# Two head pairs transposed through f32 PSUM instead of bf16 PSUM, in a fused attention and SwiGLU kernel

## The chip, the cores and the metric

The kernel runs on one core of one Trainium2 chip. The metric is the device time of one execution in microseconds (us). One execution was also taken by the hardware profiler; its engines are PE (TensorE, the matrix engine, with PEld for its weight loads), DVE (VectorE), ACT (ScalarE), POOL (GpSimd) and SP (SyncE). A matrix product reads SBUF and writes PSUM; DVE and ACT read PSUM and write SBUF.

## What is computed

The reference is attention with a squared ReLU in place of the softmax, then a root mean square norm and a SwiGLU feed-forward layer (FFN):

```python
batch, n_heads, seq, head_dim = (8, 12, 448, 64)
scores = scale * np.matmul(q, k.transpose(0, 1, 3, 2))
attn = np.maximum(scores, 0.0) ** 2 / S
attn_out = np.matmul(attn, v)

x = attn_out.transpose(0, 2, 1, 3).reshape(B * S, H * D)      # 3584 x 768
xn = x / np.sqrt(np.mean(x * x, axis=-1, keepdims=True) + 1e-06) * rms_g
g = xn @ w_gate                                               # 768 x 1536
out = (g * (1.0 / (1.0 + np.exp(-g))) * (xn @ w_val)) @ w_out # 1536 x 768
```

All inputs and the output are f32; the kernel rounds them to bf16 as it loads them and multiplies in bf16 with sums in f32.

## The kernel before

**Tiling.** The scores are computed with keys on the partitions, so that attn needs no transpose; q and k therefore have to lie with the head dimension on the partitions. The 12 heads are taken as 6 pairs j (two heads of 64 fill 128 partitions), and the tile qkT holds, per pair, 448 columns of k and 448 of q. Batch 0 is worked on in two halves of 224 query columns each (a0 and a1), the other batches in one piece of 448. The 448 keys are three blocks of 128 and a remainder of 64; the remainders of two pairs are multiplied together (tile psR). A score unit of a0 is two such blocks (tile psS, 2 x 448 columns); ReLU (lines 858 and 860) moves it to SBUF as r, and line 866 squares it there on DVE. A visit (line 1024, tile psAV) multiplies the squared scores of two pairs by v. When the three visits of a half are through, the sums of squares (psSS), their power (Ln and Exp on ACT, lines 1160 and 1164) and the scaled xn (line 1180) follow, and then the FFN products (line 147 in the profile: the planner's `slot`, tiles psg, psv and psO).

**Transposes.** q and k of batches 0 and 1 are transposed on PE, from batch 2 on by DMA. For batch 0, k of a pair is 7 pieces of 64 x 64 per head, and the first half of q is 2 pieces of 112 x 64 per head. `transposes` (lines 621 to 687) writes all 18 of a pair, with the identity tile as the other operand, into one bf16 PSUM tile psT in one of the two narrow banks, and then one copy of 672 columns, by DVE (line 677) or ACT (line 679), takes them to qkT. The function `transposes_f32` (lines 689 to 741) is in the file too, but no pair uses it while F32_T is 0. The second half of q follows later for three pairs at once.

**Start of the work.** POOL issues the loads of k, q, v and the weights one after the other; heads 0 to 3 of k are the first (line 527). The first halves of q for heads 0 to 3 and 4 to 7 come as f32 through SP's and ACT's queues, and a cast (line 1385, on ACT or DVE) brings each to bf16. PE runs fillers (tile psB, line 1532: products of a constant with itself that no one reads) whenever the planner has nothing for it, until the first FFN product is under way.

**The order** is written out when the kernel is built, by the planner (class Planner). It holds a clock of its own for each engine, with a cost for each instruction, and emits the instructions in the order in which its clock starts them; on the chip each engine runs its instructions in this order, and semaphores hold it where data is missing. An elementwise task may list two engines; `engine_next` (line 90) gives it to the engine that can start it first, then by priority, and on a tie to the engine that is listed first. PEN (line 64) is a handicap in planner nanoseconds for a ReLU on DVE:

```python
key = (s + (self.PEN if e == "dve" and "act" in cost
            and item[3].__name__ in self.acts else 0.0), prio, seq)
```

FLOOR (line 380) is a list of earliest times, by the planner's clock, at which the first eight loads of POOL's queue count as landed; the first is that of k's heads 0 to 3. The planner's narrow banks are m0 and m1, its wide tiles (two banks each) s0, s1 and s2; scores, remainders and visits take wide ones. In a choice for PE the planner looks first at visits, remainders and transposes that are ready (`choose`, line 262), then at score units, then at FFN products, and runs a filler if nothing is ready within 110 ns (GAP, line 61).

Of the kernel before, what the change touches and what calls it, by code (L numbers as in the profile page):

```python
# [54 lines left out]
class Planner:  # L55
# [5 lines left out]
    GAP = 110.0  # L61
    either = ("square", "squared")
    SLACK = 0.0
    PEN = 200.0
    acts = ("relu",)

    def __init__(self, nc, tc, banks, wide, warm):
# [22 lines left out]
    def engine_next(self):  # L90
        best = None
        for item in self.tasks:
# [4 lines left out]
            for e in cost:  # L97
# [3 lines left out]
                if item[3].__name__ in self.either and e == "act" and s + cost[e] > max(r, self.free["dve"]) + cost["dve"] + self.SLACK:  # L101
                    continue
                key = (s + (self.PEN if e == "dve" and "act" in cost and item[3].__name__ in self.acts else 0.0), prio, seq)
                if best is None or key < best[0]:
# [236 lines left out]
def kernel(  # L341
# [35 lines left out]
    JOIN = 300.0  # L377
    LAG = 2800.0
    LAG0 = 2050.0
    FLOOR = 5850.0, 8500.0, 9350.0, 10450.0, 11150.0, 11850.0, 13150.0, 14900.0  # L380
    floors = []
    LASTW = (384, 192, 192)
    A2, A3, A5 = (384, 384), (256, 256, 256), (512, 256)
# [2 lines left out]
    WO = (A2, A2, A2, A2)  # L386
    ORDER = "w0-2 w2-4 k w4-6 w6-8 w8-10 K w10-12 v"
    FIRST = "k4-8 q8-12 k8-12 v0-4 v4-12 Q"
    F32_T = 0
    AGATE = 6  # L390
    THIRD = 0
    THIRDV = 3
# [53 lines left out]
    def issue(fn, nbytes, run, need=(), rate=None, ahead=8):  # L446
# [8 lines left out]
        def go(e):  # L455
# [4 lines left out]
            lag = LAG0 if dma["t"] < 5000.0 else 1900.0 if dma["t"] < 6500.0 else LAG  # L460
            at = max(dma["t"] + lag, FLOOR[len(floors)] if len(floors) < len(FLOOR) else 0.0)
            floors.append(at)
# [977 lines left out]
    for j in range(HP):  # L1440
        if j < F32_T:
            transposes_f32(j)
# [144 lines left out]
```

## Time and profile before

| what | value |
|---|---|
| median of 4 runs | 436.49 us (435.8 to 442.32) |
| the profiled execution's own time | 436.29 us |
| its span | 434.5 us |
| PE, DVE, ACT busy | 429.5, 265.2, 251.4 us |
| granted PE clock | 1.00 of full speed |
| first transposes on PE | 6.08 us |
| first FFN product | 24.92 us |
| fillers (psB) | 78 products, the last at 24.7 us |

The profile's page gives the busy time of each engine, then the span in 40 slices with a digit for the busy share in tenths, and then the costliest groups of instructions by line. The chain that ended last follows the work back from the last instruction. A timeline row is start, duration, engine, line, operation, output<-input, shapes and number of instructions, and in brackets the idle time of the engine before it and what ended that.

### The profile page before, as it was taken

How to read it: one execution, taken by the hardware profiler on the slowest of the kernel's cores; microseconds unless marked ns; L12 is line 12 of the kernel's file. 1: busy time of each engine (PE TensorE's matmuls, PEld its weight loads, DVE VectorE, ACT ScalarE, POOL GpSimd, SP SyncE). 2: the span in 40 equal slices, each digit the busy share in tenths (PEclk: the TensorE clock that was granted, in tenths of full speed). 3: DMA queues.
4: the chain of work that ended last, by engine and by line, in shares of the span. 5: the costliest groups of instructions: out<-in, count | busy, mean ns of one | idle time of the engine just before them, and what ended most of it. 6: DMA issues, size and time to landing. Idle time of an engine off the chain costs nothing.

```text
span 434.5 us, 12552 instructions
## 1 busy us (share of the span) xinstructions
PE 429.5 (99%) x5576; PEld 314.7 (72%) x5576; DVE 265.2 (61%) x437; ACT 251.4 (58%) x356; POOL 78.3 (18%) x97
## 2 busy tenths in 40 slices
PE   8999999999999999999999999999999999999996
PEld 6688788954579755885579855795569955699996
DVE  3898984478754676657854578567854577442200
ACT  4878873576653675757743676576744567342222
POOL 8544311062260160006200440001000000000000
PEclk9999999999999999999999999999999999999999
DMA  9999999699699598169917991157103200020023
GB/s 148 193 196 197 204 192 120 142 165 126 105 160 201 110 146 57 39 132 110 124 38 159 152 158 8 38 119 99 24 18 94 74 2 2 2 74 2 2 74 109
DMA packets 134805, 44.68 MB, mean 103 GB/s; under 512 B 104096, under 2 KB 131296, under 8 KB 134752
## 3 DMA queue, kind: packets, MB, share of 16 engines
q0 software_dynamic: 94448, 24.16, 57.4%
q1 hardware_dynamic: 39808, 19.50, 21.2%
q8 instruction: 43, 0.70, 0.7%
q10 hardware_dynamic: 496, 0.24, 0.2%
q14 instruction: 10, 0.08, 0.1%
HBM read 48.76 MB, written 11.01 MB: 138 GB/s over the span
## 4 chain that ended last, share of the span: by engine, by line
PE 98%; DMA 1%; issue 0%; DVE 0%; ACT 0%; POOLq 0%
PE psO L147 26%; PE psg L147 26%; PE psv L147 26%; PE psAV L1024 9%; PE psS L917 7%; PE psT L662 2%; PE psB L1532 1%; PE psR L938 1%; DMA k<-in_k_dram 1%; PE psSS L1206 0%; PE psSS L1130 0%; DVE qkT L677 0%; ACT ost L1336 0%; POOLq L1571 0%
## 5 line engine op out<-in xcount | busy, mean ns | idle before, releaser
L147 PE MATMUL psv<-xn,wv_sb 64*128 64x448 bf16 (+1 forms) x1296 | 170.3, 329 | 0.0
L147 PE MATMUL psg<-xn,wg_sb 64*128 64x448 bf16 (+1 forms) x1296 | 170.0, 329 | 0.0
L860 ACT ACTIVATE r<-psS 128x896 bf16<-128x896 f32 x133 | 119.1, 919 | 33.5 <-PE psS L917 32.7
L147 PE MATMUL psO<-wo_sb,hT 64*128 64x384 bf16 (+2 forms) x1464 | 132.3, 310 | 0.0
L147 PEld LDWEIGHTS <-hT 64*128 64x128 bf16 x1464 | 109.9, 94 | 14.5 <-issue 2.5
L147 PEld LDWEIGHTS <-wg_sb 64*128 64x128 bf16 x1296 | 94.8, 94 | 30.6 <-issue 3.2
L147 PEld LDWEIGHTS <-wv_sb 64*128 64x128 bf16 x1296 | 93.9, 94 | 31.5 <-issue 2.5
L866 DVE TENSOR_TENSOR r<-r 128x896 bf16<-128x896 bf16 (+1 forms) x171 | 99.9, 609 | 12.1 <-ACT r L860 11.4
L1258 DVE TENSOR_TENSOR hT<-sil,psv 128x448 bf16<-128x448 bf16 x96 | 59.2, 617 | 61.4 <-PE psv L147 61.1
L1242 ACT ACTIVATE sil<-psg 128x448 bf16<-128x448 f32 x96 | 52.3, 545 | 47.8 <-PE psg L147 47.7
L917 PE MATMUL psS<-qkT 64*128 64x448 bf16 (+1 forms) x324 | 53.0, 329 | 0.1
L1336 ACT COPY ost<-psO 128x384 f32<-128x384 f32 (+2 forms) x51 | 23.0, 452 | 50.1 <-PE psO L147 50.0
L508 POOL DMA_DIRECT2D vb<-in_v_dram x18 | 13.1, 742 | 181.0 <-PE psg L147 75.6
L1024 PE MATMUL psAV<-r,vb 64*64 64x448 bf16 (+1 forms) x756 | 43.1, 335 | 0.4
L860 ACT ACTIVATE r<-psR 128x896 bf16<-128x896 f32 (+1 forms) x24 | 20.1, 839 | 28.7 <-PE psR L938 28.7
L1055 DVE TENSOR_SCALAR xT<-psAV 128x896 bf16<-128x896 f32 (+1 forms) x20 | 20.4, 1021 | 25.9 <-PE psAV L1024 25.8
L1180 DVE SCALAR_TENSOR_TENSOR xn<-xT,g_sb,rstd 128x448 bf16<-128x448 bf16 (+1 forms) x54 | 30.2, 627 | 7.8 <-ACT rstd L1164 7.7
L555 POOL DMA_DIRECT2D kb<-in_k_dram x42 | 31.5, 799 | 13.7 <-DMA vb<-in_v_dram 6.3
L1024 PEld LDWEIGHTS <-vb 64*64 64x64 bf16 x756 | 18.5, 105 | 20.6 <-PE psAV L1024 8.5
L917 PEld LDWEIGHTS <-qkT 64*128 64x128 bf16 x324 | 19.2, 94 | 9.8 <-issue 1.1
L858 DVE TENSOR_SCALAR r<-psS 128x896 bf16<-128x896 f32 x11 | 12.0, 1088 | 17.6 <-PE psS L917 17.4
L1080 DVE TENSOR_TENSOR x2f<-xT 128x896 f32<-128x896 bf16 x19 | 20.6, 1084 | 2.0 <-ACT xT L1053 2.0
(49 smaller groups left out, 174.6 us busy)
## 6 DMA issues: line engine op xcount, KB each, us to landing
vb<-in_v_dram POOLq DMA_DIRECT2D x14, 384.0 KB, 6.4
kb<-in_k_dram POOLq DMA_DIRECT2D x42, 96.0 KB, 7.2
qb<-in_q_dram POOLq DMA_DIRECT2D x6, 672.0 KB, 9.8
out_dram<-ost SPq DMA_DIRECT2D x7, 336.0 KB, 2.8
wg_sb<-in_moe_w_gate_dram POOLq DMA_DIRECT2D x6, 384.0 KB, 13.2
wv_sb<-in_moe_w_val_dram POOLq DMA_DIRECT2D x6, 384.0 KB, 13.2
wo_sb<-in_moe_w_out_dram POOLq DMA_DIRECT2D x2, 1152.0 KB, 19.2
out_dram<-ost SPq DMA_DIRECT2D x8, 288.0 KB, 2.9
```

The lines of the kernel that those rows point to most:

```text
L147: mm = self.nc.tensor.matmul(out=seg.bank["tile"][:, off : off + seg.w], lhsT=lhsT[prt], rhs=rhs[prt], start=(seg.first and h == 0 and i = ...
L555: lambda o=o, i=i: nc.gpsimd.dma_start(out=o, in_=i),
L860: nc.scalar.activation(out=r[:, :, :w], in_=ps[:, :, :w], func=ACT.Relu)
L866: nc.vector.tensor_tensor(out=r[:, :, :w], in0=r[:, :, :w], in1=r[:, :, :w], op=ALU.mult)
L917: nc.tensor.matmul(out=ps[:, hh, o : o + n], lhsT=t[prt, j, 0, c * P : (c + 1) * P], rhs=t[prt, j, 1, sub.q0 : sub.q0 + n], start=True, st ...
L1024: mm = nc.tensor.matmul(out=ps[hh * D : (hh + 1) * D, jj, :n], lhsT=vt[prt, 2 * (ja + jj) + hh, u * D : (u + 1) * D], rhs=r[prt, hh, o : o ...
L1055: nc.vector.tensor_scalar_mul(out=xT[at], in0=ps[:, :, :n], scalar1=inv_attn)
L1080: nc.vector.tensor_tensor(out=got["x2"][:], in0=xT[at], in1=xT[at], op=ALU.mult)
L1180: nc.vector.scalar_tensor_tensor(out=xn[:, kt, q0 : q0 + n], in0=xTs[b, 0][:, kt, q0 : q0 + n], scalar=g_sb[:, kt : kt + 1], in1=rstd[:, q ...
L1242: nc.scalar.activation(out=s[:, :m], in_=ps[:, :m], func=ACT.Silu)
L1258: nc.vector.tensor_tensor(out=h[:, fbs[0] : fbs[-1] + 1, o : o + n], in0=s[:, :m].rearrange("p (f s) -> p f s", s=n), in1=ps[:, :m].rearra ...
L1336: nc.scalar.copy(out=ost[:, c0 : c0 + w], in_=ps[:, :w])
```

## The change

The first two pairs of batch 0 take the function `transposes_f32` instead of `transposes`; the handicap of a ReLU on DVE goes from 200 to 100, and the first landing time from 5850 to 6000.

```diff
-    PEN = 200.0
+    PEN = 100.0
...
-    FLOOR = 5850.0, 8500.0, 9350.0, 10450.0, 11150.0, 11850.0, 13150.0, 14900.0
+    FLOOR = 6000.0, 8500.0, 9350.0, 10450.0, 11150.0, 11850.0, 13150.0, 14900.0
...
-    F32_T = 0
+    F32_T = 2
```

The function that is now called, in its core:

```python
def run(s):
    bank = take_wide()
    ps = bank.take("psT")                       # f32, 2 x 512 columns
    parts = (
        ("k", [(u, D, u % UH * P + u // UH * D) for u in range(U)], S),
        ("q", [(c, PC, c * PC) for c in range(2)], 2 * PC),
    )
    for i, (nm, steps, width) in enumerate(parts):
        for c, w, o in steps:
            for hh in range(2):
                nc.tensor.matmul(
                    out=ps[hh * D : (hh + 1) * D, i, o : o + w],
                    lhsT=ld[nm, 0][:w, 2 * j + hh, c * D : (c + 1) * D],
                    rhs=ident[:w, :w], start=True, stop=True,
                )
        s += 2.0 * sum(w / 2.4 + 2.5 for _, w, _ in steps)
        def copy(e, i=i, width=width):
            (nc.vector.tensor_copy if e == "dve" else nc.scalar.copy)(
                out=t[:, j, i, :width], in_=ps[:, i, :width])
        pl.task(2, {"dve": dve_cost(width), "act": act_cost(width)}, copy,
                [Tok(s + 200.0)], done[i], over)
    return s + pl.SW
```

Instead of the transpose mode with a bf16 result, these are ordinary products with the identity, with f32 results; k goes to the first bank of a wide PSUM tile and q to its second bank. There are two copies, one of k's 448 columns and one of q's 224, each with its own readiness, and each may go to DVE or to ACT. The calls in batch 0 are unchanged:

```python
for j in range(HP):
    if j < F32_T:
        transposes_f32(j)
    else:
        transposes(0, [j], 0, 2, True)
```

## The prediction

> **What bounds the kernel now.** I read the page's busy line first, then the chain that ended last in order of time, then the timeline of the first 25 us, then the groups by shape. The page says that TensorE (PE) is busy for almost the whole span:
>
> ```profile
> span 434.5 us, 12552 instructions
> ...
> PE 429.5 (99%) x5576; PEld 314.7 (72%) x5576; DVE 265.2 (61%) x437; ACT 251.4 (58%) x356; POOL 78.3 (18%) x97
> ...
> PEclk9999999999999999999999999999999999999999
> ```
>
> A busy PE is not a useful PE, though. The tile psB is filler: products of ones that no one reads. The chain between 5 and 25 us shows where fillers stand on the path. Columns are start, length, what:
>
> ```profile
> 1.25 4.79 DMA k<-in_k_dram
> ...
> 6.08 1.18 PE psT L662 x36
> 7.26 0.30 PE psB L1532 x2
> 7.56 0.30 PE psS L917 x4
> 7.86 0.30 PE psB L1532 x2
> ...
> 23.20 1.78 PE psB L1532 x17
> ```
>
> From 6.08 us on, the psB pieces of that chain sum to 0.30 + 0.30 + 0.20 + 0.41 + 0.69 + 1.11 + 0.20 + 0.50 + 0.50 + 1.78 = 5.99 us. After 24.9 us, where the first FFN product runs, there is no psB at all, and PE is busy 34.94 of the 35.00 us from 25 to 60 and 299.87 of the 300 us from 100 to 400. So all of the PE's real work after the first FFN product has to be done anyway, and **the only time that an edit of the first stage can win is those 5.99 us**, of which the last 1.78 wait for the scale of the first half (Ln, Exp, table load, xn), not for transposes. What holds the fillers up is DVE and ACT: from 10 to 14 us they are busy 3.88 and 3.56 of 4.00 us. The timeline at the edit itself:
>
> ```profile
> 6.75 0.51 DVE L677 COPY qkT<-psT 128x672 bf16<-128x672 bf16 x1 [5.22 <-PE psT L662]
> ...
> 7.30 0.72 ACT L679 COPY qkT<-psT 128x672 bf16<-128x672 bf16 x1 [3.10 <-PE psT L662]
> 7.48 0.43 DVE L1385 CAST qb<-qf 112x512 bf16<-112x512 f32 x1 [0.23 <-DMA qf<-in_q_dram]
> 7.49 0.11 PEld L917 LDWEIGHTS <-qkT 64*128 64x128 bf16 x4 [0.18 <-DVE qkT L677]
> ...
> 7.92 1.75 ACT L860 ACTIVATE r<-psS 128x896 bf16<-128x896 f32 x2
> ```
>
> Here the bracket is the idle time before the instruction and who ended it. Pair 0 is copied by DVE at 6.75 to 7.26, its scores start at 7.49; pair 1 is copied by ACT at 7.30 to 8.02, and the remainder scores psR, which need both pairs, start at 8.12.
>
> **The change, part by part.** *TensorE.* Per pair 14 products for k and 4 for q, of the same tile sizes (64*64 and 112*64), instead of as many transposes. Before, the 14 k issue from 6.08 to 6.42 and the 4 q from 6.42 to 6.63, 0.55 us a pair. The products are not in the trace. Below I take 0.55 us: the weight loads of the 14 k sum to 0.30 us and stay, so there is nearly nothing to gain. Above: the q transposes issue every 0.21/4 = 52 ns for 112 columns, 0.47 ns a column; 64 columns at that rate without overlap are 30 ns, 14 of them 0.42 instead of 0.34 us, so +0.08 a pair, +0.16 us for both. I take +0, since the AV products with the same 64*64 tiles and f32 out issue 16 in 0.46 us with 224 columns each, far more overlap than is needed here.
>
> The row for the engine clock: the granted clock is 1.00 in every window that I asked. [...]
>
> *Copies.* One copy of 672 bf16 columns becomes a copy of 448 and one of 224 f32 columns. Rows by shape for reading f32 PSUM: DVE 128x448 takes 0.624, 128x896 1.088, so 1.04 ns a column and 224 columns an estimated 0.39; ACT 128x448 takes 0.543, 128x896 0.919, so 224 columns an estimated 0.355, with the 128x224 Ln row at 0.441 as the upper end. Which engine gets which follows from the planner's rule (the engine that can start first, on a tie the one listed first, DVE for copies, ACT for the cast) and its own clock, used for order alone: k of pair 0 goes to DVE, q to ACT; the second q cast, due at 7.4, finds both engines free and now goes to **ACT** instead of DVE; k of pair 1 goes to DVE, and its q, with ACT in the cast, **also to DVE**, behind k.
>
> In trace time: k0 can start when the 14 k of pair 0 end (6.08 + 0.41, and 0.04 as before): DVE 6.53 to 7.15; q0 ACT 6.75 to 7.11. Scores of unit 0, with the 0.23 us seen from copy end to score, at 7.38 instead of 7.49: **-0.11**. k1 DVE 7.10 to 7.72 (neighbours overlap by some 0.05). Cast ACT 7.48 (its data land then) to 8.10, 0.617 by its row. q1 DVE 7.70 to 8.09. So pair 1 is whole at 8.09 instead of 8.02: **+0.07**, and ACT is free for the first relu at about 8.02 instead of 7.92: **+0.10**; DVE is free at 8.09 instead of 7.91. In sum of engine time, 0.51 + 0.72 + 0.43 = 1.66 us become 2 x 0.624 + 0.355 + 0.39 + 0.617 = 2.61 us; q0 and the head start of k0 lie in idle time, the rest doesn't.
>
> *What is queued behind it.* The planner fills PE until pair 1 is ready by its clock, which now counts about 6 fillers (96 ns each) where there were 2. On the chip: unit 0 issues 7.38 to 7.68, 6 fillers to 8.28, the 0.19 us change of tile mode seen in front of psR, psR at 8.47 instead of 8.12: **+0.35**. By then pairs 2 and 3 are due and stand before the second unit, so that unit's relu, at 8.80 to 9.67 on ACT today, moves behind a copy, to about 10.2; the remainder's relu (0.54 on ACT) takes its place. Engines catch up part of that, as they idle 0.39 (ACT, before 10.06) and 0.55 (DVE, before 8.46) now, and PE runs the two transposes of pairs 2 and 3 at the same time as before. I carry the 0.35 of psR to the end, as DVE and ACT are near full until 18 us: below -0.11 (the lead of unit 0, all else absorbed), above +1.2 (the 0.35 and a whole relu, 0.919, that finds no idle time).
>
> *Wide banks.* The two pairs take two of the three wide PSUM tiles, free again at 7.15 and 8.09; unit 0 takes the third at 7.38, psR the first, so nothing waits; pairs 2 and 3 find both narrow banks unused, but they wait for their k anyway (issued 2.80, landing 5.5 to 6.0 later).
>
> *First landing time 6000 instead of 5850, tie weight 100 instead of 200.* Both change only written order. The landing itself (6.04) stays, and 27 fillers precede it either way. A relu now goes to DVE when it can start there over 0.1 us sooner instead of 0.2 (14 of 171 went there). One moved relu costs DVE 1.088 and frees ACT 0.919; the cover is PE's full queue after 25 us (34.94 of 35.00), so 0 there; in 10 to 25 us it is worth between -0.5 (half an idle relu slot: DVE idles 0.43 from 14 to 18 and 1.33 from 18 to 21) and +0.17 (1.088 - 0.919). I take 0, since the engines are nearly equally loaded.
>
> *Sum:* the profiled execution took 436.29 us, its span 434.5 and 1.79 around it; 436.29 + 0.35 = **436.64**. The median of the four runs shown, 436.49, is 0.20 higher, so 436.7 as a round figure between the two bases. A measurement can't tell a change of under 1% (4.4 us) from none here in the sense of the chances below.
>
> **The rivals.** (1) *Faster.* The cast stays on DVE or lands late, q1 goes to ACT at 7.30 to 7.66, and pair 1 is whole at k1's end, 7.72: -0.30 against 8.02; with the -0.5 of the tie weight 436.29 - 0.8 = 435.5. For it: ACT idled 3.10 us before its first copy. Against: by the planner's rule both engines are free at 7.4. (2) *The work lost is a whole relu round:* +1.2, 437.5. For it: DVE 3.88 of 4.00 busy from 10 to 14. (3) *Slower by over 1%: VectorE becomes the bound from 25 to 60 us.* It is busy 31.06 of 35.00 there, 3.94 spare; 21 relus run on ACT in that window. From the fourth that moves (3.94/1.088 = 3.6) each adds 1.088 us: with 9 moved 9 x 1.088 - 3.94 = 5.85, 442.1. For it: the tie weight pushes exactly this way. Against: the planner moves a relu only where DVE can start sooner, and the FFN products let PE run on. (4) *It does not do what it says:* pair 1 is not split between engines, as derived above, and the f32 form buys nothing; that is inside the forecast, 436.3 to 436.7.
>
> **How the numbers follow.** Forecast with (4), 436.2 to 437.2: 0.50. Rival 1: 0.23. Rival 2: 0.23. Rival 3: 0.04. The range runs from rival 1 at 435.5 to rival 2 with the products' +0.16 and the base's 0.20, 437.9; outside stay rival 3 and the tails of the other two. Faster by over 1% would need 4.4 of the 4.21 us of fillers (5.99 - 1.78) that transposes can touch: 0.01. Slower by over 1% is rival 3: 0.04.
>
> **What would show it.** Right: a DVE copy of 448 f32 columns starting near 6.5 and a second near 7.1, an ACT copy of 224 between them; the cast on ACT near 7.5; psR later than 8.12; six fillers before it; the first FFN product at 24.9 to 25.6 instead of 24.92. Wrong: psR before 8.0, psB in the chain under 5.5 us after 6.08 (rival 1); psB over 7 (rival 2); PE idle by more than 1 us between 25 and 60 with DVE over 34 of 35 busy (rival 3).

## The result

The median of the changed kernel is 439.8 us (44 executions, 436.54 to 443.54), that of the kernel before 436.54 us (63 executions, 435.80 to 443.82). The ratio is 1.005 with a 95% interval of 1.0031 to 1.0068: slower by some half per cent, and outside the forecast range of 435.5 to 437.9. (The ratio leaves out the most disturbed executions of both kernels; the medians are of all of them.)

The median hides what happened. Each execution has a mean granted TensorE clock, and the changed kernel's times fall into groups by it: 17 executions at 0.998 to 1.000 take 436.54 to 437.41 us (median 436.92), 13 at 0.990 to 0.991 take 439.66 to 440.45, and 14 at 0.983 to 0.988 take 440.94 to 443.54. So 27 of 44 lost clock. The kernel before has the slower groups too, but 13 of 63 times (counted here by a time over 439 us); its others have a median of 436.50. "Low clock" below means a mean granted clock under 0.995. Two numbers have to be explained: **+0.42 us** between executions at full clock, and **the share of low clock, from 13 of 63 to 27 of 44**.

The profiled execution of the changed kernel (437.01 us) is one at full clock. Its page:

```profile
span 435.2 us, 12562 instructions
...
PE 429.7 (99%) x5582; PEld 315.6 (73%) x5582; DVE 266.8 (61%) x438; ACT 250.9 (58%) x357; POOL 78.2 (18%) x97
...
PEclk9999999999999999999999999999999999999999
```

The timeline at the edit (start, duration, engine, line, operation, shapes, and in brackets the idle time before and who ended it):

```profile
6.09 0.41 PE L721 MATMUL psT<-ident,k 64*64 64x64 bf16 x14 [0.36 <-DMA k<-in_k_dram]
...
6.76 1.18 DVE L731 CAST qkT<-psT 128x448 bf16<-128x448 f32 x2 [5.25 <-PE psT L721]
...
7.42 0.34 ACT L731 CAST qkT<-psT 128x224 bf16<-128x224 f32 x1 [3.18 <-DVE qkT L731]
...
7.82 0.37 PE L917 MATMUL psS<-qkT 64*128 64x224 bf16 x4 [0.54 <-ACT qkT L731]
...
8.22 2.14 DVE L858 TENSOR_SCALAR r<-psS 128x896 bf16<-128x896 f32 x2 [0.28 <-PE psS L917]
...
8.64 0.29 PE L938 MATMUL psR<-qkT 64*64 64x224 bf16 x4
```

Two waits stand here that the forecast didn't have. The copy of k starts at 6.76, when the products of q have ended, not at 6.53, when those of k have. And the copy of q on ScalarE was released by **VectorE's copy of k**, not by TensorE: the two copies, meant to run side by side, run one after the other. TensorE then has nothing to do for 0.54 us, and the first scores start at 7.82 instead of 7.49. The same chain as the one shown of before, from the first k to the first FFN product:

```profile
6.76 0.64 DVE qkT L731
...
7.42 0.35 ACT qkT L731
...
8.18 0.41 PE psB L1532 x3
8.60 0.04 issue
8.64 0.29 PE psR L938 x4
...
13.05 1.60 PE psB L1532 x15
...
25.85 0.20 PE psg L147
```

Two lines of the chain of before, to set beside the last two:

```profile
13.37 0.69 PE psB L1532 x6
...
24.98 0.20 PE psg L147
```

The transposes' copies are now on the path for 0.99 us; by this chain the first FFN product comes at 25.85 instead of 24.98, and the span is 0.7 us longer.

### The profile page after: what moved, and what is told of

Same layout as the page of the kernel before. It is cut to its first block, busy times and chain, and to the rows that moved or that the text cites. A ratio compares the mean times of both kernels' runs of the same rounds, so it can differ in the third digit from the quotient of the medians.

```text
span 435.2 us, 12562 instructions
## 1 busy us (share of the span) xinstructions
PE 429.7 (99%) x5582; PEld 315.6 (73%) x5582; DVE 266.8 (61%) x438; ACT 250.9 (58%) x357; POOL 78.2 (18%) x97
## 4 chain that ended last, share of the span: by engine, by line
PE 98%; DMA 1%; issue 0%; ACT 0%; DVE 0%; POOLq 0%
PE psO L147 26%; PE psg L147 26%; PE psv L147 26%; PE psAV L1024 9%; PE psS L917 7%; PE psB L1532 1%; PE psT L662 1%; PE psR L938 1%; DMA k<-in_k_dram 1%; PE psSS L1206 0%; PE psSS L1130 0%; PE psT L721 0%; DVE qkT L731 0%; ACT qkT L731 0%; ACT ost L1336 0%
## 5 line engine op out<-in xcount | busy, mean ns | idle before, releaser
L860 ACT ACTIVATE r<-psS 128x896 bf16<-128x896 f32 x131 | 117.3, 919 | 33.0 <-PE psS L917 32.1
L860 ACT ACTIVATE r<-psR 128x896 bf16<-128x896 f32 (+1 forms) x26 | 21.6, 831 | 32.1 <-PE psR L938 32.1
L1055 DVE TENSOR_SCALAR xT<-psAV 128x896 bf16<-128x896 f32 (+1 forms) x21 | 21.5, 1024 | 27.7 <-PE psAV L1024 27.6
L1024 PEld LDWEIGHTS <-vb 64*64 64x64 bf16 x756 | 18.6, 105 | 20.4 <-PE psAV L1024 8.3
L858 DVE TENSOR_SCALAR r<-psS 128x896 bf16<-128x896 f32 x13 | 14.1, 1089 | 16.9 <-PE psS L917 16.7
```

The source lines that it names most:

```text
L860: nc.scalar.activation(out=r[:, :, :w], in_=ps[:, :, :w], func=ACT.Relu)
L1024: mm = nc.tensor.matmul(out=ps[hh * D : (hh + 1) * D, jj, :n], lhsT=vt[prt, 2 * (ja + jj) + hh, u * D : (u + 1) * D], rhs=r[prt, hh, o : o ...
L1055: nc.vector.tensor_scalar_mul(out=xT[at], in0=ps[:, :, :n], scalar1=inv_attn)
```

## The experiments

Each kernel ran in five rounds beside the kernel before on the same chip. Of the kernel before, low clock came in 2 of 31, 7 of 28, 3 of 29 and 7 of 29 executions in the four sets, and the medians of its executions at full clock were 436.19, 436.43, 436.40 and 436.41 us. Differences below are against the set's own.

**The changed kernel again**, first beside the next three kernels and a second time in the last set.

> The changed kernel once more, for the spread of its times and, with luck, a profile of an execution with a granted TensorE clock below 1. So far its times fall into three groups: 436.5 to 437.4 us (clock 0.998 to 1.000), 439.7 to 440.5 (0.990 to 0.991) and 440.9 to 443.5 (0.983 to 0.988). Theory C (clock gate): the upper groups are one or two stretches at half clock, started by TensorE's pause of 0.54 us after the first transposes; then the profile shows a clock below 0.95 in one or two of the first slices (0 to 25 us) and full clock after, and over 40% of executions are above 439 us. Rival R1 (chance): the kernel before has such executions as often once enough are taken side by side; then both show the same share above 439 us.

> The changed kernel beside the two others on the same chip: 40 to 65% of executions below clock 0.995, median 437 to 441 us, the others at 436.5 to 437.4. If the share is a property of the chip (rival R7), it can be under 20% here, and then the two others say nothing.

Measured: 6 of 12 and 8 of 12 at low clock; at full clock medians of 436.86 (+0.67) and 436.93 (+0.51). With the first 44 that is 41 of 68, against 32 of 180 of the kernel before, and on both chips the kernel before beside it had far fewer (2 of 31 and 7 of 29): the share is the kernel's own, not chance and not the chip. The first of these two runs was profiled in a low-clock execution (442.75 us). TensorE by stretches of 2.5 us (stretch, its length and busy time, instructions, granted clock, DMA share, GB/s):

```profile
5.00:7.50 2.50, 1.27 (x27) 1.00 1.32 212
7.50:10.00 2.50, 1.90 (x33) 0.69 1.37 190
10.00:12.50 2.50, 2.50 (x46) 0.50 1.45 195
12.50:15.00 2.50, 2.44 (x41) 0.50 1.72 186
15.00:17.50 2.50, 2.50 (x31) 0.50 1.48 197
17.50:20.00 2.50, 2.44 (x33) 0.76 1.46 197
20.00:22.50 2.50, 2.44 (x46) 1.00 1.79 189
```

The clock is at half for (1 - 0.69)/0.5 x 2.5 = 1.55 us of the second stretch, all of the next three, and 1.2 us of the sixth: 10.25 us in one piece, from 8.45 us on, **right after the stretch in which TensorE was least busy** (1.27 of 2.50 us); in every later stretch up to 50 us it is 1.00. In this execution the first k landed late as well, so that TensorE paused 1.23 us in front of the transposes and 0.54 us behind them:

```profile
6.93 0.41 PE L721 MATMUL psT<-ident,k 64*64 64x64 bf16 x14 [1.23 <-DMA k<-in_k_dram]
...
8.65 0.56 PE L917 MATMUL psS<-qkT 64*128 64x224 bf16 x4 [0.54 <-ACT qkT L731]
```

The low-clock profile of the second run (441.22 us) has the same two pauses, the first of them short:

```profile
6.32 0.41 PE L721 MATMUL psT<-ident,k 64*64 64x64 bf16 x14 [0.28 <-DMA k<-in_k_dram]
...
8.04 0.37 PE L917 MATMUL psS<-qkT 64*128 64x224 bf16 x4 [0.54 <-ACT qkT L731]
```

That is no more pause than the full-clock profile has (0.36 and 0.54). The runs below show the low clock more or less often as the pauses change (0 of 10 executions with the second one filled, 41 of 68 with it); the length of the pauses does not decide it for a single execution.

**The parts of the change alone.**

```diff
 # the f32 form alone
-    PEN = 100.0
+    PEN = 200.0
-    FLOOR = 6000.0, ...
+    FLOOR = 5850.0, ...
 # the weights alone
-    F32_T = 2
+    F32_T = 0
```

> F32_T = 2 alone, with the tie weight at 200 and the first landing time at 5850. If the new copies and waits are the cause (theory C and the lost 0.45 us), it behaves like the changed kernel: undisturbed executions at 436.7 to 437.3 us, and over 25% of all executions above 439 us. If the refitted weights are the cause (rival R2), it is like the kernel before: 436.3 to 436.7, under 25% above 439 us.

> Tie weight 100 and first landing time 6000 alone, with F32_T = 0. Theory C: like the kernel before, 436.2 to 436.8 us and under 25% of executions above 439 us. Rival R2 (the weights do it): 436.7 to 437.3 us and over 25% above 439 us.

Measured: the f32 form alone 438.22 us at full clock (**+2.0**), 3 of 8 at low clock. The weights alone 436.95 (**+0.75**), 1 of 11 at low clock. Both times lie above what theory C expected; that of the weights is what rival R2 had, without its share of over 25%. The shares point to the f32 form as the source of the low clock, though 8 and 11 executions are few. At full clock both parts cost, the two together (+0.67) less than either: the new weights repair most of what the f32 form costs with the old ones, and nothing of its wait (0.54 us in the profile of the f32 form alone too). The weights alone write 84 fillers where the kernel before has 78. Their profile kept full clock (0.998) in spite of a long pause in front:

```profile
6.15 0.41 PE L662 MATMUL psT<-ident,k 64*64 64x64 bf16 x14 [1.18 <-DMA k<-in_k_dram]
```

**Two PSUM tiles: the wait between the copies taken away.**

```diff
-            bank = take_wide()
-            ps = bank.take("psT")
+            bank, qbank = take_wide(), take_bank()
+            tiles = [bank.take("psT")[:, 0, :], qbank.take("psTq")]
...
-                            out=ps[hh * D : (hh + 1) * D, i, o : o + w],
+                            out=tiles[i][hh * D : (hh + 1) * D, o : o + w],
...
-                        out=t[:, j, i, :width], in_=ps[:, i, :width]
+                        out=t[:, j, i, :width], in_=tiles[i][:, :width]
```

> The changed kernel with q's products in a PSUM tile of their own (a narrow bank), so that q's copy on ScalarE waits for TensorE and no longer for VectorE's copy of k. Theory C with the wait as its start: q0 is copied at 6.76 to 7.11 beside k0 (6.53 to 7.15), scores start near 7.4 instead of 7.82, TensorE's pause shrinks from 0.54 to under 0.2 us, undisturbed executions fall by 0.3 to 0.5 us to 436.3 to 436.7, and the share above 439 us falls below 30%. Rival R3 (written order, not the wait, sets both): scores start earlier but the fillers eat it, times stay at 436.7 to 437.2 and the share above 439 us stays over 40%.

Measured: 436.65 us at full clock (+0.46, where the changed kernel on this chip has +0.67), and **0 of 11** at low clock. The timeline:

```profile
6.23 0.44 PE L715 MATMUL psT<-ident,k 64*64 64x64 bf16 x14
6.60 0.29 PE L715 MATMUL psTq<-ident,qb 112*64 112x112 bf16 x4
6.71 1.18 DVE L725 CAST qkT<-psT 128x448 bf16<-128x448 f32 x2 [5.19 <-PE psT L715]
...
6.93 0.35 ACT L725 CAST qkT<-psTq 128x224 bf16<-128x224 f32 x1 [2.83 <-PE psTq L715]
...
7.40 0.37 PE L911 MATMUL psS<-qkT 64*128 64x224 bf16 x4
```

Now k's copy starts 0.04 us after k's own products end (6.23 + 0.44), q's copy is released by TensorE and runs beside it, and the scores start at 7.40, 1.17 after the first product instead of 1.73. Both waits of the changed kernel came from the shared tile. The time at full clock moved by 0.2 us only, against the 0.3 to 0.5 expected: most of that part has another cause.

**The pause filled, the waits left.** Three fillers behind the second pair's products, everything else as in the changed kernel.

```diff
+            if j == F32_T - 1:
+                for _ in range(3):
+                    pl.fill()
             return s + pl.SW
```

> The changed kernel with three fillers written behind the products of the second pair and nothing else moved: the copies and the wait of ScalarE for VectorE stay, only TensorE works in place of pausing (its pause of 0.54 us before the first scores should fall below 0.1). Theory C (the pause starts the half clock): executions with a clock below 0.995 fall from half to under 20%, median 436.8 to 437.2 us. Rival R4 (the delay of the scores, or the products themselves, start it): still 40 to 60% below 0.995, median over 438.

```profile
7.21 0.47 PE L1535 MATMUL psB<-const-bfloat16-1.0 128*128 128x224 bf16 x3
7.42 0.35 ACT L731 CAST qkT<-psT 128x224 bf16<-128x224 f32 x1 [3.38 <-DVE qkT L731]
...
7.82 0.37 PE L920 MATMUL psS<-qkT 64*128 64x224 bf16 x4
```

Measured: **0 of 10** at low clock, with the wait in place and the scores at 7.82 as before. It is TensorE's pause that brings the low clock (41 of 68 with it), not the late scores and not the f32 products. At full clock it takes 437.40 (+0.97), more than the 436.8 to 437.2 expected; its profiled execution (437.08) has the first FFN product at 25.86, as the changed kernel has it, so where the rest of the +0.97 lies is not shown.

**A pause made in the kernel before.** Four fillers left out, then eight.

```diff
 # four: those between the first transposes and the remainder scores
-        if self.warm() and (not times or ...):
+        if self.warm() and not 6700.0 < t < 8100.0 and (not times or ...):
 # eight: those four, and the last four in front of the first transposes
+        if count not in [24, 25, 26, 27, 28, 29, 30, 31]:
             nc.tensor.matmul(out=bank.fill, ...)
```

Here and below, `count` stands for the running number of a filler.

> The kernel before, its four fillers between the first transposes and the remainder scores left out (they stand in the plan's 6.7 to 8.1 us), nothing slower and no product with f32: TensorE pauses some 0.3 us twice. Theory C: executions with a clock below 0.995 rise from 16% to over 35%, the others stay at 436.0 to 436.7 us. Rival R4: share unchanged, below 20%.

> The kernel before with eight fillers left out: the last four in front of the first transposes and the four between them and the remainder scores. TensorE's pause for the first k grows by some 0.5 us. Theory C (pauses around the first transposes start the half clock): over 60% of executions below clock 0.995, more than the 6 of 12 with four fillers left out; the others at 436.0 to 436.7 us. Rival R4: share as in the kernel before, under 25%.

Measured: with four out 6 of 12 at low clock, the others at 436.29 (-0.14). Beside it the kernel before had 7 of 28. So the low clock comes with bf16 transposes too, and more often when TensorE pauses behind them, though 12 executions are few. With eight out all six executions take 439.94 to 443.21, where theory C had the undisturbed ones at 436.0 to 436.7; three of them have a recorded clock of 0.985 to 0.988, and three one of 1.000. The profiled one is of the second kind (440.94), and its rows tell more than its mean clock (first two rows of before, then the same two with eight left out):

```profile
6.08 0.41 PE L662 MATMUL psT<-ident,k 64*64 64x64 bf16 x14 [0.47 <-DMA k<-in_k_dram]
6.42 0.29 PE L662 MATMUL psT<-ident,qb 112*64 112x112 bf16 x4
```

```profile
6.04 0.58 PE L662 MATMUL psT<-ident,k 64*64 64x64 bf16 x14 [0.81 <-DMA k<-in_k_dram]
6.55 0.40 PE L662 MATMUL psT<-ident,qb 112*64 112x112 bf16 x4
```

The 14 transposes of k took 0.58 us here and 0.41 in the profile of before, the 4 of q 0.40 and 0.29; none of the 23 fillers in front took less than 345 ns, where those of before reach 261. Their median is 391 ns, as in the first 5 us of before; the later ones of before have 262. TensorE was still slow at 16.7 us, where six fillers take 1.24 us, and no longer at 20.4, where ten take 1.10:

```profile
16.69 1.24 PE psB L1534 x6
...
20.35 1.10 PE psB L1534 x10
```

So this kernel shows a slow pace that lasts from the start to some 20 us, rather than a fall from the faster one. That the four fillers missing in front bring it is a reading: no run leaves out those alone.

**More work in front of the first transposes.** Five more fillers there, in the kernel before and in the changed one.

```diff
 # kernel before
+            if b == 0 and with_k and pairs[0] == 0:
 # changed kernel
+            if j == 0:
 # both
+                for _ in range(6):
+                    pl.fill()
```

Six are asked for, and five more stand in front of the transposes in the profiles (32 instead of 27, and 33 instead of 28); `fill` writes none when no bank is free.

> The kernel before with five more fillers written in front of the first transposes, so that TensorE works on until about 6.2 us instead of 5.6. Theory C: share below clock 0.995 under 8% (22 of 122 in the kernel before), and the others lose at most what the fillers overrun k's landing at 6.04: 436.3 to 436.9 us. Rival R7 (the share is set by the chip and the landing of k, not by the pause): 10 to 30% below 0.995.

> The changed kernel with five more fillers in front of the first transposes; the pause of 0.54 us behind them, the copies and the wait stay. If the two pauses add up (theory C, in its form that the half clock comes when TensorE works too little between 5 and 9 us as a whole): share below clock 0.995 falls from 33 of 56 to under 25%, the others at 436.8 to 437.3 us. If the pause behind the transposes alone decides (rival C2): still 40 to 65%.

Measured: the kernel before with them has **0 of 11** at low clock and a median of 436.48 (+0.08 at full clock); as the kernel before had only 3 of 29 on that chip, this says little alone. The changed kernel with them has 2 of 12, beside 8 of 12 without them on the same chip, and 437.67 at full clock (+1.26, more than expected, not explained). The fillers cover a part of the pause in front (0.40 us in the profile of the kernel before with them, 0.47 without, k landing 0.06 us later), but they don't remove it: in a low-clock profile of the changed kernel with them it is still 0.95 us, as k landed late.

```profile
6.71 0.41 PE L724 MATMUL psT<-ident,k 64*64 64x64 bf16 x14 [0.95 <-DMA k<-in_k_dram]
```

More work in front, with the 0.54 us behind left in place, takes most of the low clock away; removing the pause behind, by fillers or by two tiles, took nearly all of it (0 of 10 and 0 of 11, and 1 of 6 and 0 of 11 in the two further forms with two tiles below). Both pauses count.

The landing of k, which no edit here touches, seems to have a part in it. The first transposes start at 6.22 to 7.32 us in the six profiles whose clock falls. Of the ten with a mean granted clock of 0.997 to 1.000 (that with eight fillers left out aside), they start at 5.92 to 6.23 in eight; the other two are 6.45 in a form with two tiles and, by its chain, 6.89 behind fillers that left no pause.

**The +0.42 at full clock: fillers that the plan writes.** On TensorE the order is written in advance, fillers included, and each issues in 0.1 us (15 in 1.60 in the chain of the changed kernel). In front of the first FFN product the kernel before has 78, the changed one 84, the f32 form alone 87. Five of the 15 in front of the changed kernel's first visit (six in the kernel before) were left out:

```diff
+        if count not in range(43, 48):
             nc.tensor.matmul(out=bank.fill, ...)
```

> The changed kernel with the last 5 of the 15 fillers in front of the first visit left out, all else in the same order. Theory O (fillers written by plan stand on the path): visit 0 starts 0.3 to 0.5 us sooner than 14.57 and the undisturbed executions fall from 436.9 to 436.3 to 436.6 us. Rival R6 (the data of the visit, squares on VectorE, are late anyway): TensorE waits there as long as the fillers took and the time stays at 436.7 to 437.2 us. Clock share: like the changed kernel, 40 to 60%, since the first pause is untouched.

```profile
12.90 1.16 PE L1534 MATMUL psB<-const-bfloat16-1.0 128*128 128x224 bf16 x10
14.01 0.58 PE L1024 MATMUL psAV<-r,vb 64*64 64x224 bf16 x16
```

Measured: the visit's first product at 14.01 instead of 14.70 (0.09 of that is the earlier landing of k), and 436.66 at full clock (+0.23), just above the 436.3 to 436.6 expected. Low clock in 5 of 12. The squares were there; TensorE was running fillers over data that it could have used. The changed kernel did not run beside it on this chip; against its +0.42 to +0.67 in other sets, some 0.2 to 0.4 us is won.

> Two PSUM tiles as in the earlier run, with tie weight 200 and first landing time 5850. Theory O (written order sets the undisturbed time: this one writes 87 fillers, the changed kernel 84, the kernel before 78, at 0.1 us each): 437.2 to 438.3 us, near the f32 form alone with one tile (438.25). Rival R5 (the wait for VectorE sets it): 436.0 to 436.6 us. Share below clock 0.995 under 20% by theory C, as TensorE no longer waits for a copy.

Measured: two tiles with the old weights 437.86 at full clock (+1.43), 1 of 6 low. The wait is gone and the time is still near that of the f32 form alone (+2.0), which has the same 87 fillers in the same places: the written order sets most of it. Nine more fillers at 0.1 us are 0.9 us, so their number alone does not make up the +1.43; what else of the order costs is not shown.

**Fewer fillers in other places**, to find a version that beats both: 14 out in the kernel before, 17 out in the form with two tiles.

```diff
+        if count not in [41, 42, 49, 50, 51, 52, 57, 61, 73, ..., 78]:                  # kernel before
+        if count not in [43, ..., 47, 54, 55, 56, 57, 63, 67, 79, ..., 84]:             # two tiles
             nc.tensor.matmul(out=bank.fill, ...)
```

> The kernel before with 14 of its 51 later fillers left out (2 of 6 before the first visit, 4 of 10 before the second, 1 of 4 twice, 6 of 17 before the first FFN product), all else in the same order. Theory O (fillers written by plan stand on the path): undisturbed executions 0.4 to 1.4 us below the kernel before, 435.0 to 436.0. Rival R6 (data are late anyway): 436.1 to 436.7. Share below clock 0.995 like the kernel before, under 25%, since the first pause is untouched.

> The changed kernel with two PSUM tiles and 17 of its later fillers left out (5 of 15, 4 of 10, 1 of 4 twice, 6 of 17). Theory O: 0.5 to 1.5 us below the form with two tiles (436.65), 435.1 to 436.1 us, and then the f32 form without its false wait and without the plan's surplus is level with the kernel before or better; share below 0.995 under 20%. Rival R6: 436.4 to 437.0 us.

Measured: the kernel before with 14 fewer takes 435.96 at full clock (-0.44), as theory O expected, but with 4 of 12 at low clock, beside 3 of 29, where under 25% was expected. Two tiles with 17 fewer takes 436.64 (+0.24, 0 of 11 low), which is what rival R6 expected: next to the +0.46 of two tiles some 0.2 us is won, not 0.5 to 1.5. The chain of the second kernel shows a wait where fillers were, on ScalarE's ReLUs:

```profile
12.53 2.98 ACT r L854 x4
15.51 0.04 issue
15.55 0.37 PE psS L911 x4
15.92 0.69 PE psB L1528 x6
16.61 0.51 PE psAV L1018 x16
```

**Both together, on the kernel before**: five more fillers in front, 14 fewer later.

> The kernel before with five more fillers in front of the first transposes and 14 fewer later (2 of 6, 4 of 10, 1 of 4 twice, 6 of 18): no half clock as in the form with more warming (0 of 11), and 0.4 us less in the undisturbed executions as in the form with fewer fillers (435.96 against 436.40): median 435.8 to 436.2 us, ahead of both kernels. If the pauses left by the missing fillers bring the half clock (rival C3): over 20% below 0.995 and a median over 436.4.

Measured: 436.15 us (435.50 to 437.46), 0 of 12 at low clock; the kernel before beside it 436.57, with 7 of 29 low. The ratio is 0.9976 with an interval of 0.9948 to 1.0005. It is the fastest median of its set, as expected, but the interval just touches 1; a sure gain is not shown. With the 0 of 11 above, the five fillers in front leave 0 of 23 executions at low clock, against 10 of 58 of the kernel before beside them.

## Why the prediction was wrong, point by point

**The failed step is the engine clock**, a term that the forecast put at nothing. It read a granted clock of 1.00 in every window of one profile and left the clock out of its sum; that there was something to lose was not asked. The times hinted at it: 442.32 among the four shown is 1.3% above the others and lies where the low-clock executions lie. The kernel before stood near an edge, 32 of 180 over it, and the change moved it further over: 41 of 68. The forecast had even written a pause down ("unit 0 issues 7.38 to 7.68", after transposes that issue until 7.2, no filler between) and priced it by its length. Its price is not its length: a low-clock execution costs some 3 to 6.5 us more (439.7 to 443.5 against 436.92). At full clock the changed kernel lies inside the range.

**Copies side by side: wrong, and this made the pause.** "k0 can start when the 14 k of pair 0 end", DVE 6.53 to 7.15 with q0 on ACT at 6.75 to 7.11, was read from the code. With one tile for both, k's copy waits for q's products and q's copy for k's. Scores started at 7.82, not 7.38, and TensorE paused 0.54 us. With two tiles they start at 7.40, and that kernel takes +0.46 at 0 of 11 low clock, against a forecast of +0.35: the reading was right for a kernel that isn't this one.

**The sizes of the copies: right.** 0.624 measured as taken, 224 columns on ACT 0.346 against an estimated 0.355. **The products: right**, k and q of a pair issue in 0.56 us against 0.55, at the lower end of the bounds. (In front of them stand 28 fillers, not the 27 that were to "precede it either way".) **Rival 4 was half right**: for the old weights the second pair's q does go to VectorE behind k, as derived; with the new weights it goes to ScalarE behind the cast, at 8.18.

**psR and the carry to the end: near in number, by luck.** psR at 8.64, forecast 8.47; executions at full clock +0.42, forecast +0.35. But three fillers stood there, not six, and the delay came from the wait; and what reached the end came in part from fillers further on, which the forecast did not count.

**The tie weight: mis-sized.** Taken as 0 "since the engines are nearly equally loaded"; alone, with the landing time, it costs 0.75 us, and it writes six more fillers. The first ReLU went to VectorE (8.22), not to ScalarE as worked out.

**The late rivals: excluded.** VectorE as the bound from 25 to 60 us (rival 3) does not appear: TensorE is busy 35.00 of 35.00 us there in the profile after. It was the only rival that lay wholly above the range, and it named the wrong engine.

## What to carry to other kernels

Before an edit of a kernel's first microseconds, look at the spread of its times: a second group 0.6 to 1.5% up with a lower granted clock (0.983 to 0.991) meant here that TensorE was near a pause that costs far more than it lasts (0.54 us, and an execution some 3 to 6.5 us longer); the edit's pauses must then be seen together with those already there, a late first load among them. Fillers in front of the first real work were a cheap cover for it in the kernel before (+0.08 us), though not in the changed one (+1.26), while fillers written into the order where data may be early are work on the path (the first visit at 14.01 us instead of 14.70 with five fewer). Two engines that read one tile were put in order here even though they touch different parts of it: ScalarE's copy of q started at 7.42, released by VectorE's copy of k, and at 6.93 beside it when q had a tile of its own; look at what released the second one, or give each its own tile.

## What the runs showed of the hardware

Six profiles have a mean granted clock under 0.995, and in the first 25 us of each the clock is at half in one piece. A stretch of 2.5 us with a granted clock of c has (1 - c)/0.5 x 2.5 us at half; from the two stretches at the edges of the piece (start, granted clock), to some 0.03 us:

| profile | first stretch | last stretch | half from | full again | half for |
|---|---|---|---|---|---|
| changed kernel, first run above | 7.5, 0.69 | 17.5, 0.76 | 8.45 | 18.70 | 10.25 |
| changed kernel, second run | 7.5, 0.84 | 17.5, 0.62 | 9.20 | 19.40 | 10.20 |
| f32 form alone | 7.5, 0.77 | 17.5, 0.69 | 8.85 | 19.05 | 10.20 |
| four fillers left out of before | 7.5, 0.62 | 20.0, 0.65 | 8.10 | 21.75 | 13.65 |
| two tiles, old weights | 5.0, 0.93 | 20.0, 0.84 | 7.15 | 20.80 | 13.65 |
| changed kernel, more fillers in front | 10.0, 0.69 | 17.5, 0.94 | 10.95 | 17.80 | 6.85 |

So half clock stood for 6.85 us in one of them, 10.20 to 10.25 in three and 13.65 in two. Why these lengths is not shown.

How much work keeps the clock is not shown either. From 5.0 to 7.5 us TensorE is busy for 0.59 to 2.21 us in the six; for 1.92 in the full-clock profile of the changed kernel and 2.03 in that of the kernel before. Busy time by itself does not separate them. Nor does the longest pause: in two of the six (the second run of the changed kernel and the f32 form alone) none was longer than 0.54 us, and the weights alone kept full clock with one of 1.18.

That the three groups of times answer to the three lengths fits their sizes: half of 6.85, 10.2 and 13.65 us is 3.4, 5.1 and 6.8, and among the first 44 executions the medians at clocks of 0.990 to 0.991, 0.986 to 0.988 and 0.983 to 0.984 lie 2.9, 4.6 and 6.3 us above those at full clock. The lengths themselves were seen only in the executions that were profiled.

A granted clock of 1.00 is not always one pace. It stands over the first 5 us of the profiles of the kernel before and of the changed one, where the fillers take 391 and 394 ns in the median, and after 5.2 us, where they take 262. With eight fillers left out it stands over every stretch up to 22.5 us, the slow fillers at 16.7 us among them, and the mean is 1.000 for an execution of 440.94 us.
